# Converting the second weight chunk in two pieces, w3's rows ahead of w_out's, in a fused attention and feed-forward kernel

## The chip, the cores and the metric

The kernel runs on one core of a Trainium2 chip. The metric is the device time of one execution in microseconds (us). "Before" is the kernel without the change, "after" the kernel with it.

## The reference, cut to what matters

```python
# attention: q, k, v of 8 x 8 x 576 x 64
kv  = einsum('bhsd,bhse->bhde', k, v)
out = einsum('bhsd,bhde->bhse', q, kv)
out = out / sqrt(mean(out*out, -1) + 1e-6) * g_norm
x   = out rearranged to (4608, 512)
# feed-forward: w1, w2 (512, 1024); w3 (1024, 1024); w_out (1024, 512)
h = ((x @ w1) * (x @ w2)) @ w3
return h @ w_out
```

The weights arrive as 64-bit floats and are converted to fp32 on the chip.

## The kernel before, as far as it matters here

The kernel first folds w3 and w_out into one matrix, so that the last two products become one. It does so in two halves of w3's rows. In the first half it walks through eight chunks. One chunk is 512 columns of raw w3 data and 512 of raw w_out data per partition, loaded by two transfers of 512 KB, w3 first. Per chunk:

1. **Conversion.** ScalarE does two operations (L147, L148), VectorE four (L150, L154, L157, L160).
2. **Transpose of w3's part** on TensorE (L443) and its copy out of PSUM by ScalarE (L448).
3. **Fold** on TensorE (L456): four products of the transposed w3 with w_out, seen as eight passes in the profile. Three of the products (six passes) stand ahead of the next chunk's transpose, the fourth behind it.

TensorE, ScalarE and VectorE each work through their operations in the order in which the program was written.

```python
    def conversion(n, dst, raw, cols=slice(0, 1024)):
        # ... (views of the two 32-bit halves of each value)
        nc.scalar.activation(low, lo, AF.Copy, scale=2.0 ** -51, bias=2.0)      # L147
        nc.scalar.activation(dst, hi.bitcast(FP32), AF.Abs)                     # L148
        yield
        nc.vector.scalar_tensor_tensor(...)                                     # L150
        nc.vector.tensor_scalar(out=dst, in0=dst, scalar1=LEAST, scalar2=MOST,  # L154
                                op0=ALU.max, op1=ALU.min)
        nc.vector.tensor_scalar(...logical_shift_left)                          # L157
        nc.vector.tensor_tensor(out=dst_bits, in0=dst_bits, in1=low_bits, ...)  # L160
    # ...
    def conversions(n):
        # ...
        dst = chunks[:, i].rearrange("p w f -> p (w f)")   # w3's 512 columns, then w_out's
        cuts = [0, 1024] if i else [0, 256, 512, 1024]
        return [conversion(n, dst, raws[n], slice(a, b)) for a, b in zip(cuts, cuts[1:])]
    # begin_next(): the ScalarE part of the next chunk; end_next(): its VectorE part
    # ...
        keep_warm(14)              # matmuls on the identity, so that TensorE is not idle
        begin_next()
        end_next()                 # chunk 0
        turn_w3(0, 0)              # transposes L443, copy L448
        keep_warm(5)
        begin_next()               # chunk 1
        # ...
        for c in range(KF):
            if c == 0:
                end_next()         # chunk 1
                begin_next()       # chunk 2
            else:
                begin_next()
                end_next()
            # ...
            fold_chunk(0, c, range(NH - 1))
            turn_w3(*((0, c + 1) if c + 1 < KF else (1, 0)))
            fold_chunk(0, c, [NH - 1])
```

## Time and profile before

| | before |
|---|---|
| median of the first 3 runs | 814.15 us (813.13 to 815.48) |
| span of the profiled execution | 811.6 us |
| TensorE busy | 803.0 us (99%) |
| VectorE, ScalarE busy | 363.6 us, 266.8 us |
| TensorE's longest wait | 2.73 us, for the conversion of chunk 1 |

The prediction shows the lines for this. One view that it does not show is the chain of work that ended last, followed back from the end of the program. These are its pieces around the wait (start us, duration us, what):

```profile
3.27 6.86 DMA raw<-in_moe_w_out_dram
...
10.21 1.14 ACT ab L147
11.37 1.23 DVE ab L150
...
13.96 1.24 DVE chunks L160
...
15.24 0.66 PE at L443 x4
```

The chain runs from chunk 1's w_out transfer through its conversion into the transpose. From 15.24 on it is TensorE alone. In what follows **"the third transpose batch"** is the one of chunk 2, at 19.25 us here. It is a good marker: from it to the end of the span this profile takes 811.6 - 19.25 = 792.35 us.

### The profile page before, as it was taken

To read this page: it belongs to the slowest core of one execution; us is meant where nothing else is said; L and a number is where in the kernel's file an instruction comes from. 1 tells how busy PE (TensorE), PEld (TensorE's weight loads), DVE (VectorE), ACT (ScalarE), POOL (GpSimd) and SP (SyncE) were. 2 spreads that over 40 slices of the span, in tenths; PEclk is the share of its full clock that TensorE was granted. 3 is DMA by queue.
4 is the path that set the end of the run, shared out by engine and by line. 5 is a ranking of instruction groups with operands and counts; after the bars stand their busy time and mean duration, and the time that the engine had idled before them with its cause. 6 is when DMAs were issued, how large, how long until landed. Compare 5 with 4: busy or idle time off the path is not lost.

```text
span 811.6 us, 12588 instructions
## 1 busy us (share of the span) xinstructions
PE 803.0 (99%) x5335; PEld 676.8 (83%) x5335; DVE 363.6 (45%) x680; ACT 266.8 (33%) x501; POOL 1.8 (0%) x8
## 2 busy tenths in 40 slices
PE   7999999999999999999999999999999999999998
PEld 5455788888888888888888888888888888888887
DVE  6958998324522453155315531543154415422431
ACT  6677743124312431233124322331234212211220
POOL 0000000000000000000000000000000000000000
PEclk9999999999999999999999999999999999999999
DMA  9996433032003210312032202120210010002001
GB/s 322 332 328 182 146 91 92 1 131 82 10 1 130 75 31 1 119 47 56 1 103 67 66 1 85 56 82 0 79 52 1 1 52 1 0 1 53 1 0 53
DMA packets 60811, 59.53 MB, mean 73 GB/s; under 512 B 15316, under 2 KB 57300, under 8 KB 60756
## 3 DMA queue, kind: packets, MB, share of 16 engines
q1 hardware_dynamic: 60608, 58.60, 23.2%
q8 instruction: 42, 0.69, 0.4%
q14 instruction: 13, 0.11, 0.0%
q10 hardware_dynamic: 148, 0.13, 0.0%
HBM read 49.28 MB, written 9.44 MB: 72 GB/s over the span
## 4 chain that ended last, share of the span: by engine, by line
PE 98%; DMA 1%; DVE 0%; SPq 0%; ACT 0%; issue 0%; ACTq 0%
PE mm L471 81%; PE mm L456 7%; PE at L275 3%; PE at L345 2%; PE at L294 2%; PE at L378 2%; DMA raw<-in_moe_w_out_dram 1%; PE at L443 1%; PE at L363 0%; SPq L183 0%; PE at L387 0%; PE at L304 0%; DVE chunks L160 0%; DVE ab L150 0%; ACT ab L147 0%
## 5 line engine op out<-in xcount | busy, mean ns | idle before, releaser
L471 PE MATMUL mm<-xT,w_sb 128*128 128x256 f32 x768 | 176.2, 379 | 0.0
L471 PEld LDWEIGHTS mm<-xT,w_sb 128*128 128x128 f32 x768 | 146.0, 190 | 20.2 <-issue 0.5
L471 PE MATMUL mm<-xc,ws 128*128 128x256 f32 x576 | 130.2, 379 | 0.0
L471 PEld LDWEIGHTS mm<-xc,ws 128*128 128x128 f32 x576 | 109.5, 190 | 14.8
L484 ACT COPY u<-mm 128x512 f32<-128x512 f32 x90 | 52.7, 585 | 206.0 <-PE mm L471 185.9
L484 ACT COPY p<-mm 128x512 f32<-128x512 f32 x90 | 52.7, 586 | 134.4 <-PE mm L471 134.4
L471 PE MATMUL mm<-w3o_sb,ab 128*128 128x256 f32 x432 | 96.2, 379 | 0.0
L597 DVE TENSOR_TENSOR c<-mm,u 128x512 f32<-128x512 f32 x36 | 24.8, 689 | 157.3 <-PE mm L471 157.3
L471 PEld LDWEIGHTS mm<-w3o_sb,ab 128*128 128x128 f32 x432 | 82.1, 190 | 11.1
L471 PE MATMUL mm<-xc,w_sb 128*128 128x256 f32 x288 | 68.9, 382 | 0.0
L471 PE MATMUL mm<-raw 128*128 128x256 f32 x288 | 63.6, 379 | 0.0
L471 PE MATMUL mm<-xT,ws 128*128 128x256 f32 x256 | 61.6, 383 | 0.0
L471 PEld LDWEIGHTS mm<-raw 128*128 128x128 f32 x288 | 54.8, 190 | 7.4
L456 PE MATMUL mm<-chunks,ab 128*128 128x512 f32 x128 | 60.0, 601 | 0.2 <-DVE chunks L160 0.2
L471 PEld LDWEIGHTS mm<-xc,w_sb 128*128 128x128 f32 x288 | 52.8, 190 | 6.9 <-ACT u L484 0.3
L471 PEld LDWEIGHTS mm<-xT,ws 128*128 128x128 f32 x256 | 46.7, 190 | 6.0
L314 DVE TENSOR_REDUCE inv<-sq 128x8 f32<-128x512 f32 (+1 forms) x40 | 23.5, 626 | 58.4 <-ACT sq L313 58.4
L598 DVE TENSOR_TENSOR ab<-c 128x256 f32<-128x256 f32 x108 | 45.4, 421 | 2.9
L638 DVE TENSOR_TENSOR raw<-mm,u 128x512 f32<-128x512 f32 x8 | 5.5, 692 | 83.4 <-PE mm L471 72.7
L456 PEld LDWEIGHTS mm<-chunks,ab 128*128 128x128 f32 x128 | 21.9, 190 | 21.6 <-issue 16.1
L597 DVE TENSOR_TENSOR c<-p,u 128x512 f32<-128x512 f32 x36 | 24.9, 691 | 28.4 <-ACT u L484 28.1
L471 PE MATMUL mm<-w3o_sb,raw 128*128 128x256 f32 x144 | 32.7, 380 | 0.0
(90 smaller groups left out, 769.3 us busy)
## 6 DMA issues: line engine op xcount, KB each, us to landing
raw<-in_moe_w_dram SPq DMA_DIRECT2D x31, 512.0 KB, 7.0
k_sb<-in_k_dram SPq DMA_DIRECT2D x32, 256.0 KB, 3.9
v_sb<-in_v_dram SPq DMA_DIRECT2D x32, 256.0 KB, 4.4
q_sb<-in_q_dram SPq DMA_DIRECT2D x32, 256.0 KB, 4.5
out_dram<-raw SPq DMA_DIRECT2D x14, 512.0 KB, 2.6
raw<-in_moe_w_out_dram SPq DMA_DIRECT2D x7, 512.0 KB, 7.7
out_dram<-raw SPq DMA_DIRECT2D x9, 128.0 KB, 2.4
kl_sb<-in_k_dram SPq DMA_DIRECT2D x8, 128.0 KB, 4.8
```

What stands on the lines that cost most here:

```text
L275: nc.tensor.matmul(kv_ps[e * D:(e + 1) * D, r - rs[0], :], lhsT=k_sb[:, e, cols] if j < J else kl[:, 2 * r + e, :], rhs=v_sb[:, e, cols] i ...
L294: nc.tensor.transpose(qt_ps[:, e, i, :], q_sb[:, e, i * P:(i + 1) * P], ident)
L314: nc.vector.tensor_reduce(out=inv[:, i], in_=sq.rearrange("p (h d) -> p h d", d=D), axis=AX.X, op=ALU.add)
L345: nc.tensor.matmul(o_ps[l][tokens, n * D:(n + 1) * D], lhsT=qT[r][rows, e, i, tokens], rhs=kv_b[rows, e, r, :], start=True, stop=True,)
L378: nc.tensor.transpose(t_ps[:, j, :], st[r // 2][:, j // 2, j % 2, m:m + 2, :], ident)
L443: nc.tensor.transpose(t_ps[:, m, :], src, ident)
L456: nc.tensor.matmul(sums_ps[half][m], lhsT=w3T[half, c][:, m, :], rhs=chunks[:, c, 1, :], start=(c == 0), stop=(c == KF - 1),)
L471: nc.tensor.matmul(ps[:, u, :], lhsT=lhsT(a_name, u, c), rhs=rhs(b_name, c),  start=(u == 0 and c == 0 and to is None), stop=(c == chunks ...
L484: nc.scalar.copy(t, ps)
L597: nc.vector.tensor_add(c, one, two)
L598: nc.vector.tensor_mul(dst, c[:, 0, :], c[:, 1, :])
L638: nc.vector.tensor_add(dst, one, two)
```

## The change

The transpose needs only w3's part of the chunk, yet the conversion waits for both transfers. The change cuts chunk 1's conversion in two, w3 first, so that the w3 piece can start one transfer earlier.

```diff
-        cuts = [0, 1024] if i else [0, 256, 512, 1024]
+        cuts = [[0, 256, 512, 1024], [0, 512, 1024], [0, 1024]][min(i, 2)]
```

## The prediction

> **What bounds the kernel now.** I read the page's span and busy shares first, then everything TensorE waited for in the whole run, then the timeline of the first 25 us by engine, then when the transfers issued there landed.
>
> ```profile
> span 811.6 us, 12588 instructions
> PE 803.0 (99%) x5335; PEld 676.8 (83%) x5335; DVE 363.6 (45%) x680; ACT 266.8 (33%) x501; POOL 1.8 (0%) x8
> ...
> PE at L443 <- DVE chunks L160: 2.7, 1, 2.7
> PE mm L256 <- POOL ident masks.py:199: 1.9, 1, 1.9
> PE mm L456 <- DVE chunks L160: 0.2, 1, 0.2
> ```
>
> The first two lines say that TensorE is the bound: 803.0 of 811.6 us. The last three are all the waits of TensorE that the trace has, with total, count and longest. One wait of 2.7 us is worth attacking: a transpose (L443) of w3 chunk 1 that waits for the last conversion step (L160) of that chunk. The granted clock is 1.00 in every stretch I read, so one stretch can be compared with another by time. After this wait TensorE has no gap to the end. So what the change saves is read from when TensorE gets going again, near 15 us; later stages can only take it back.
>
> The three engines there (start us, duration us, engine, line; idle time before it and its releaser in brackets):
>
> ```profile
> 9.70 2.81 PE L456 MATMUL mm<-chunks,ab 128*128 128x512 f32 x6 [0.22 <-DVE chunks L160]
> 15.24 0.66 PE L443 MATMUL at<-ident,chunks 128*128 128x128 f32 x4 [2.73 <-DVE chunks L160]
> 15.74 3.68 PE L456 MATMUL mm<-chunks,ab 128*128 128x512 f32 x8
> ```
> ```profile
> 8.26 0.59 ACT L448 COPY ab<-at 128x512 f32<-128x512 f32 x1 [0.37 <-PE at L443]
> 10.21 1.13 ACT L147 ACTIVATE ab<-raw 128x1024 f32<-128x1024 uint32 x1 [1.37 <-DMA raw<-in_moe_w_out_dram]
> 11.25 1.14 ACT L148 ACTIVATE chunks<-raw 128x1024 f32<-128x1024 f32 x1
> ...
> 13.02 1.14 ACT L147 ACTIVATE ab<-raw 128x1024 f32<-128x1024 uint32 x1 [0.59 <-DMA raw<-in_moe_w_out_dram]
> 14.06 1.13 ACT L148 ACTIVATE chunks<-raw 128x1024 f32<-128x1024 f32 x1
> 15.94 0.58 ACT L448 COPY ab<-at 128x512 f32<-128x512 f32 x1 [0.74 <-PE at L443]
> ```
> ```profile
> 7.34 0.69 DVE L150 SCALAR_TENSOR_TENSOR ab<-raw,ab 128x512 uint32<-128x512 uint32 x1 [0.19 <-ACT ab L147]
> ...
> 8.87 0.69 DVE L160 CUSTOM_DVE_ANT_0 chunks<-chunks,ab 128x1024 uint16<-128x1024 uint16 x1
> 11.37 1.23 DVE L150 SCALAR_TENSOR_TENSOR ab<-raw,ab 128x1024 uint32<-128x1024 uint32 x1 [1.81 <-ACT ab L147]
> ...
> 13.96 1.22 DVE L160 CUSTOM_DVE_ANT_0 chunks<-chunks,ab 128x2048 uint16<-128x2048 uint16 x1
> 15.11 1.22 DVE L150 SCALAR_TENSOR_TENSOR ab<-raw,ab 128x1024 uint32<-128x1024 uint32 x1
> ```
>
> Chunk 1's conversion starts at 10.21, when the w_out half has landed, though the transpose needs only the w3 half. ScalarE takes L147 and L148, VectorE then L150, L154, L157 and L160, to 15.18; the transpose runs at 15.24. The line to keep in view is ScalarE's at 15.94: it copies the transposed w3 chunk 1 out, it stands in ScalarE's order behind chunk 2's L147 and L148, and these had waited until 13.02 for chunk 2's own w_out.
>
> Landings, each window holding one issue (last column: us from issue to landing). The issues were at 2.79 (chunk 1, w3), 3.27 (chunk 1, w_out) and 5.26 (chunk 2, w_out):
>
> ```profile
> raw<-in_moe_w_dram SPq DMA_DIRECT2D x1, 512.0 KB, 6.0
> ...
> raw<-in_moe_w_out_dram SPq DMA_DIRECT2D x1, 512.0 KB, 6.9
> ...
> raw<-in_moe_w_out_dram SPq DMA_DIRECT2D x1, 512.0 KB, 7.7
> ```
>
> So w3 of chunk 1 lands at 8.8, its w_out at 10.2, chunk 2's w_out at 13.0.
>
> **What the Trainium skill says.** "VectorE: DVE Perf Modes", section "The TRN2 errata", has a fixed cost per instruction on VectorE and ScalarE that small tiles pay each time. The trace agrees: L150 takes 1222 ns at 1024 values and 692 at 512, so 530 are for 512 values and 162 are fixed. "PSUM — Partial Sum Buffer", section "Engine vs sequencer instructions": ScalarE's and VectorE's queues are strict FIFO. ScalarE's lines agree, L448 always follows the next chunk's L148; my result hangs on this. "TensorE: Matmul & The Clock Gate", section "HAM oscillation", warns of idle gaps above about 3.4 us; the gap here is 2.73 us and the matmuls behind it take 593 ns as those ahead, so shortening it wins no clock. "DMA: Bandwidth & Descriptors", section "Where 436 GB/s comes from", puts the port ceiling at 435 GB/s; the core moved 377 to 386 GB/s from 7.5 to 15.3 us with its DMA engines always busy, so chunk 2 will not land earlier for the asking.
>
> **The change part by part.** It adds six instructions for chunk 1 (two on ScalarE, four on VectorE) and removes none of the work. By chunk 0's piece of 512, a piece costs ScalarE 6.64 to 7.89 = 1.25 us and VectorE 7.34 to 9.56 = 2.22 us. Two pieces cost ScalarE 2.50 instead of 2.18 (10.21 to 12.39) and VectorE 4.44 instead of 3.81 (11.37 to 15.18). What it moves:
>
> 1. The w3 piece on ScalarE starts when w3 has landed (8.8) and L448 of chunk 0 is done (8.85): 8.88. VectorE can begin at 8.88 + 0.69 = 9.57, just when it is done with chunk 0 (9.56). It ends at 9.57 + 2.22 = 11.8 instead of 15.18: 3.4 us earlier.
> 2. TensorE's six passes before the transpose, issued every 0.43 us from 9.70, end near 12.3. The transpose no longer waits, and runs about 2.9 us earlier. The last quarter of chunk 0's fold follows it, to about 13.6 (0.44 + 0.86).
> 3. The w_out piece on ScalarE runs 10.2 to 11.45, on VectorE 11.7 to 13.95. It is there before it can be used.
> 4. Chunk 1's fold needs the copy L448. ScalarE is in chunk 2's conversion, which still cannot start before 13.02 and ends at 15.19. So L448 runs at 15.10 (overlapping by the usual 0.1) to 15.69 instead of 15.94 to 16.52. The weight load behind it was at 16.57, and will be at about 15.74. **Gain at this point: 0.83 us**, not 2.7. TensorE's wait becomes some 1.9 to 2.1 us (13.7 to 15.75) and changes its releaser.
> 5. Does the 0.83 survive? VectorE's chunk 2 starts at 14.17 (ScalarE's L147 done, 13.02 + 1.14) instead of 15.11, ends near 18.0; its transpose comes at 19.25 - 0.83 = 18.4. Slack 0.4, as before. Chunk 3: ScalarE could start after 15.69, its data is there near 15.8 by my estimate (1 MB per 2.8 us after chunk 2's 13.0, from the two w_out landings), so VectorE gets it at about 17.0, earlier than it is free (17.9). From there VectorE takes 3.73 us a chunk (15.11 to 18.83 to 22.57) and TensorE 3.96 (15.24, 19.25, 23.21), so VectorE only pulls ahead. Loads of later chunks land in 5 to 8 us and are issued over 10 us ahead; ScalarE shows no DMA wait after 13.02. The later work of ScalarE and VectorE is released by TensorE's own results and moves with it.
>
> Sum: -0.83 us in 812, or 0.1%. From the median 814.15: 813.3.
>
> **The rivals.** (A) The whole 2.7 us goes: 811.4. For it: only one wait of that size is on record and the diff removes its releaser. Against it: L448's place behind chunk 2's L148, which the wait list cannot show, because before the change that wait is hidden under the transpose's. (B) Nothing goes, 814.1: the 0.63 us more on VectorE would count if VectorE were the pacer, as it is nearly full from 15 to 40 us. Against it: VectorE idles 1.81 us ahead of chunk 1, and the added time falls into that; it starts chunk 2 earlier than before. (C) Chunk 2 or 3 lands later, since DMA is saturated, and takes the rest back. Chunk 2's loads are issued before anything changes, so only ordinary scatter of landings remains; half a microsecond would halve the gain. (D) Slower: I see no path for it beyond scatter.
>
> **Range and chances.** The three runs of before span 813.13 to 815.48, far more than the gain, so scatter sets the range: about 1 us around the median either way, plus half a microsecond for the mechanism. 812.0 to 814.6 covers rival B and most of A. A change of 2% is 16 us; nothing here reaches it. Faster 0.005, same 0.99, slower 0.005.
>
> **What would show it right or wrong.** The wait of L443 for L160 should be gone, and a wait of about 2 us of chunk 1's first fold matmul (L456) for ACT L448 should stand in its place. L148 of 128x512 should start near 9.5; four VectorE operations of 512 values should end near 11.8; the copy L448 of chunk 1 near 15.1; TensorE's third batch of transposes (chunk 2) near 18.4; busy time of TensorE unchanged at 803. If that third batch comes at 16.5 or 19.2, step 4 or 5 is wrong. A fold start much before 15.7 would mean that ScalarE's order is not what I read. If chunk 2's first L147 starts well off 13.02, the landing moved and the size of the gain with it.

## The result

| | before | after |
|---|---|---|
| median of 6 runs | 813.75 us (813.13 to 815.48) | 812.48 us (811.69 to 814.45) |
| span of the profiled execution | 811.6 us | 809.9 us |
| third transpose batch starts | 19.25 us | 17.53 us |
| from there to the end | 792.35 us | 792.37 us |

The ratio is 0.9984 with a 95% interval of 0.9970 to 0.9999. A ratio is the mean time of one kernel's runs over that of the other's in the same rounds, so it is not quite the ratio of the medians. By the 2% rule the two are the same. The interval just excludes 1. The last row places the whole difference of the two profiles ahead of the third transpose batch.

The chain that ended last, in the profile after:

```profile
4.58 7.44 DMA raw<-in_moe_w_out_dram
...
12.12 1.17 ACT ab L147
13.29 1.03 ACT chunks L148
14.33 0.48 ACT ab L448
...
14.85 2.84 PE mm L456 x6
```

Chunk 1's w_out and all of VectorE have left the chain. It now starts at chunk 2's w_out, runs through chunk 2's two ScalarE operations to the copy of chunk 1's transpose (L448) and then to chunk 1's fold: the order that step 4 of the prediction rests on.

ScalarE's timeline after, chunk 1's w3 piece and then the copy:

```profile
8.01 0.68 ACT L147 ACTIVATE ab<-raw 128x512 f32<-128x512 uint32 x1
8.59 0.66 ACT L148 ACTIVATE chunks<-raw 128x512 f32<-128x512 f32 x1
...
14.22 0.57 ACT L448 COPY ab<-at 128x512 f32<-128x512 f32 x1
```

TensorE's timeline after, transposes and fold of chunk 1, then the third batch:

```profile
12.11 0.60 PE L443 MATMUL at<-ident,chunks 128*128 128x128 f32 x4
...
14.85 2.84 PE L456 MATMUL mm<-chunks,ab 128*128 128x512 f32 x6 [1.28 <-ACT ab L448]
17.53 0.60 PE L443 MATMUL at<-ident,chunks 128*128 128x128 f32 x4
```

VectorE's timeline after, the end of chunk 1's w_out piece and the start of chunk 2:

```profile
12.87 0.69 DVE L160 CUSTOM_DVE_ANT_0 chunks<-chunks,ab 128x1024 uint16<-128x1024 uint16 x1
13.48 1.22 DVE L150 SCALAR_TENSOR_TENSOR ab<-raw,ab 128x1024 uint32<-128x1024 uint32 x1
```

The w3 piece starts at 8.01 instead of 10.21, and the transpose at 12.11 instead of 15.24, without a wait. The 2.73 us wait has become one of 1.28 us with another releaser. The third batch moved by 1.72 us, though, which is twice the predicted 0.83. Either the landings were different or something is missing from the account. The times scatter by more than the effect, so the experiments rest on profiles first.

### The profile page after: what moved, and what is told of

Read it like the earlier page. It is cut to its first block, busy times and chain, and to the rows that moved or that the text cites. A ratio compares the mean times of both kernels' runs of the same rounds, so it can differ in the third digit from the quotient of the medians.

```text
span 809.9 us, 12595 instructions
## 1 busy us (share of the span) xinstructions
PE 802.1 (99%) x5335; PEld 675.6 (83%) x5335; DVE 363.9 (45%) x684; ACT 266.9 (33%) x503; POOL 1.8 (0%) x8
## 4 chain that ended last, share of the span: by engine, by line
PE 98%; DMA 1%; ACT 0%; issue 0%; SPq 0%; ACTq 0%
PE mm L471 81%; PE mm L456 7%; PE at L275 3%; PE at L345 2%; PE at L294 2%; PE at L378 2%; DMA raw<-in_moe_w_out_dram 1%; PE at L443 1%; DMA raw<-in_moe_w_dram 0%; PE at L363 0%; PE at L304 0%; PE at L387 0%; ACT ab L147 0%; ACT chunks L148 0%; ACT ab L448 0%
## 5 line engine op out<-in xcount | busy, mean ns | idle before, releaser
L484 ACT COPY u<-mm 128x512 f32<-128x512 f32 x90 | 52.7, 585 | 205.8 <-PE mm L471 185.9
L484 ACT COPY p<-mm 128x512 f32<-128x512 f32 x90 | 52.7, 586 | 134.4 <-PE mm L471 134.4
```

The source lines that it names most:

```text
L484: nc.scalar.copy(t, ps)
```

## The experiments

Every batch ran on one chip and shared its runs of before. The stated runs include each kernel's profiled one.

| kernel | median us (runs) | ratio to before | runs with mean granted clock of 0.998 or less |
|---|---|---|---|
| before_again | 813.67 (6) | 0.9993 | 1 of 6 |
| after_again | 812.89 (6) | 0.9984 | 2 of 6 |
| wout_first | 814.45 (6) | 0.9993 | 4 of 6 |
| copy_early | 813.16 (6) | 0.9983 | 0 of 6 |
| copy_between | 812.70 (5) | 0.9975 | 0 of 5 |
| split_c2 | 812.56 (6) | 0.9975 | 0 of 6 |
| split_all | 814.30 (6) | 0.9999 | 0 of 6 |
| after_third | 812.52 (6) | 0.9973 | 0 of 6 |
| before_third | 814.23 (6) | 1.0000 | 3 of 6 |
| fill_before | 813.76 (5) | 0.9993 | 0 of 5 |
| fill_after | 812.82 (5) | 0.9980 | 0 of 5 |
| long_gap | 818.33 (5) | 1.0050 | 5 of 5 |

All gave correct results, and by the 2% rule all are the same as before. The 95% intervals reach 0.0012 to 0.0018 to either side of a ratio, so the ratios of 0.9973 to 0.9984 can't be told apart. "Undisturbed" below means a run with a clock of 0.999 or 1.000.

### Both kernels again: where the landings fall

No edit.

> The kernel before, unchanged, for the scatter of the transfers and of the times. Ratio 1.000 to itself, interval within 0.15%. My account says that the third batch of transposes (L443, chunk 2) starts 9.1 us after chunk 1's w_out has landed (19.25 - 10.15 in the first profile), wherever that landing falls; a landing that is earlier by 0.5 us moves everything by 0.5 us. If the 1.7 us between the two first profiles is half scatter, this profile's third batch can lie anywhere between 18.3 and 19.5. The rival, that the change itself made the transfers land earlier, wants it at 19.2 to 19.3 again.

> The changed kernel, unchanged. My account: the third batch of transposes starts 5.5 us after chunk 2's w_out has landed (17.53 - 12.02), unless VectorE is the later one; ratio to before 0.9985 to 0.9995 (gain 0.4 to 1.2 us, 0.83 expected). The rival, that the change makes transfers land earlier and is worth 1.3 to 1.7 us, wants 0.9980 to 0.9984 and the landing of chunk 2's w_out near 12.0 again.

> The changed kernel a third time, for its scatter. My account: the third batch of transposes at the later of chunk 2's w_out landing + 5.5 and the end of VectorE's chunk 2; ratio to before 0.9985 to 0.9995. The rival (worth 1.3 us or more) wants 0.998.

Measured, all taken from the timelines. The start of chunk 2's first L147 stands in for the landing of its w_out; it is up to 0.1 us after it.

| profile | chunk 2's L147 | third batch | difference |
|---|---|---|---|
| before | 13.02 | 19.25 | 6.23 |
| before_again | 13.49 | 19.73 | 6.24 |
| after | 12.12 | 17.53 | 5.41 |
| after_again | 13.09 | 18.60 | 5.51 |
| after_third | 12.95 | 18.32 | 5.37 |

Before the change the third batch hangs on chunk 1's w_out: it came 9.04 and 9.05 us after chunk 1's L147 (10.21 and 10.68), as expected. That of before_again lay at 19.73, outside the 18.3 to 19.5 that I gave, because its landings were late. Chunk 2's L147 followed chunk 1's by 2.81 us in both profiles, so it can serve as the mark for both kernels.

At equal landings the change moves the third batch by 6.23 - 5.43 (mean of three) = **0.80 us**, against 0.83 predicted. The other 0.9 us between the two first profiles is the landing, 12.12 against 13.02. after_again and after_third had 13.09 and 12.95, so the change does not bring the landing forward by that much; that rival falls. A shift of a few tenths these few profiles can't exclude. In after_third, whose landing is nearest to that of before, the copy L448 runs at 15.03 (predicted 15.1), and TensorE waits 2.33 us for it (predicted some 1.9 to 2.1).

The ratios of 0.9984 and 0.9973 were lower than the 0.9985 to 0.9995 that I expected. Both intervals (0.9968 to 1.0001 and 0.9958 to 0.9988) reach into that range, but the excess came up in every batch. It is taken up below.

### w_out's piece first: early w3, or the split?

```diff
+        pieces = list(zip(cuts, cuts[1:]))
+        if i == 1:
+            pieces.reverse()
```

> Chunk 1 in the same two pieces of 512, but w_out's piece first: same instructions, no early w3. My account (it is the early w3 piece that pays, the split alone costs): the transpose of chunk 1 waits again for L160, about 0.6 us longer than before the change (two pieces of 2.2 us against 3.8 us), so the second batch of transposes at 15.9 on the first profile's landings, and the run 0.6 us slower than before, ratio 1.0007. The rival, that it is shorter instructions or the finer semaphores that help, wants 0.999 as with the change.

TensorE's timeline (the added lines move the line numbers by three):

```profile
14.96 1.12 PE L446 MATMUL at<-ident,chunks 128*128 128x128 f32 x4 [2.23 <-DVE chunks L160]
```

The transpose waits 2.23 us for the last conversion step (L160) again, and the time is that of before. So the early w3 piece is what pays. My number for the split was a miss, however: the transpose came at 14.96, 5.10 us after chunk 1's L147 (9.86), against 15.24 - 10.21 = 5.03 in before. The split costs 0.07 us, not 0.6. VectorE's two pieces take 4.34 us (10.56 to 14.90) instead of 3.81, but VectorE can begin 0.70 us after L147 starts instead of 1.16, because L147 has half the values to do. The two nearly cancel.

Another thing in this profile was unexpected. The transposes took 1.12 us instead of 0.66, the eight passes behind them 4.83 instead of 3.68, and the granted clock was 0.50 from 15.0 to 17.5 us.

### The copy ahead of chunk 2's conversion: is L448's place the only limit?

```diff
             if c == 0:
                 end_next()
+                fold_chunk(0, 0, range(NH - 1))
+                turn_w3(0, 1)
                 begin_next()
+                fold_chunk(0, 0, [NH - 1])
+                continue
```

> The changed kernel, with the copy of chunk 1's transpose (L448) ahead of chunk 2's L147 and L148 in ScalarE's order; TensorE's and VectorE's order unchanged. My account: the fold of chunk 1 starts near 13.6 to 14.0 (TensorE no longer waits about 1.3 to 2 us for that copy), but chunk 2 then starts later on ScalarE (about 13.2) and TensorE waits for VectorE's chunk 2 at the third batch of transposes, at about 18.0 to 18.3; gain against the changed kernel nil or a loss of up to 0.5 us. The rival, that the copy alone held back the rest of the 2.7 us, wants another 1 to 2 us gained: ratio to before 0.9965.

TensorE's timeline:

```profile
13.46 3.98 PE L456 MATMUL mm<-chunks,ab 128*128 128x512 f32 x8
19.28 0.63 PE L443 MATMUL at<-ident,chunks 128*128 128x128 f32 x4 [1.84 <-DVE chunks L160]
```

The wait for the copy is gone: six passes of chunk 1's fold follow chunk 0's last two within one entry. TensorE then waits 1.84 us for chunk 2, because ScalarE gave chunk 2's L147 a start of only 14.14. The third batch comes 6.7 us after the landing of chunk 2's w_out (12.6), so about 1.2 us later than with the change (5.4 to 5.5). I had expected it at 18.0 to 18.3. A part of this is the landing of chunk 0, on which the copy now hangs: its w_out was in use at 7.29 here. Against after_again, where that was even later (7.54), the third batch is still 0.68 us later (19.28 against 18.60). The undisturbed time is also worse, 813.16 against 812.51 (below). The rival, another 1 to 2 us from the copy alone, is refuted.

### The copy between chunk 2's two ScalarE operations

```diff
         nc.scalar.activation(low, lo, AF.Copy, scale=2.0 ** -51, bias=2.0)
+        if n == 2:
+            yield
         nc.scalar.activation(dst, hi.bitcast(FP32), AF.Abs)
...
                 end_next()
                 begin_next()
+                fold_chunk(0, 0, range(NH - 1))
+                turn_w3(0, 1)
+                next(begun[2][0])
+                fold_chunk(0, 0, [NH - 1])
+                continue
```

> The changed kernel, with the copy of chunk 1's transpose (L448) between chunk 2's L147 and L148 on ScalarE, so it fills ScalarE's wait without holding up chunk 2's first VectorE operation. My account (after the change ScalarE's copy and VectorE's chunk 2 bind within 0.1 to 0.3 us of each other): the fold of chunk 1 starts 1.0 us earlier than with the change, at chunk 2's w_out landing + 1.8, but TensorE then waits for VectorE's chunk 2 at the third batch of transposes, at landing + 5.4 to 5.6: nil gain, 0.0 to 0.2 us either way. The rival, that the copy is the only limit, wants the third batch at landing + 4.5 and a further 1 us.

TensorE's timeline (the added lines move the line numbers by two):

```profile
14.53 2.84 PE L458 MATMUL mm<-chunks,ab 128*128 128x512 f32 x6 [0.98 <-ACT ab L450]
18.41 0.63 PE L445 MATMUL at<-ident,chunks 128*128 128x128 f32 x4 [1.03 <-DVE chunks L162]
```

VectorE's timeline, its second operation on chunk 2:

```profile
15.58 0.69 DVE L156 TENSOR_SCALAR chunks<-chunks 128x1024 f32<-128x1024 f32 x1 [0.31 <-ACT chunks L150]
```

With the landing at 12.86 the fold starts at +1.67 instead of after's +2.7, and all of it goes back into the next wait: the third batch is at +5.55, against +5.43 with the change. The median, 812.70 against 812.52 of after_third on the same chip, says the same. A part of this the edit makes itself: chunk 2's second ScalarE operation now stands behind the copy, and VectorE waits 0.31 us for it. So this run alone does not show how near VectorE's limit lies. The profiles of after do: VectorE's chunk 2 ended 0.23, 0.14 and 0.37 us ahead of the third batch, and where TensorE waits for it the batch starts 0.14 to 0.15 us behind it (copy_early, copy_between). That leaves 0.1, 0.0 and 0.2 us. So with the change two limits lie within some 0.2 us of each other: ScalarE's copy and VectorE's chunk 2. This is why more was not to be had by moving the copy.

### Chunk 2 in two pieces as well; all chunks in two pieces

```diff
-        cuts = [[0, 256, 512, 1024], [0, 512, 1024], [0, 1024]][min(i, 2)]
+        cuts = [[0, 256, 512, 1024], [0, 512, 1024], [0, 512, 1024], [0, 1024]][min(i, 3)]   # split_c2
+        cuts = [[0, 256, 512, 1024], [0, 512, 1024]][min(i, 1)]                              # split_all
```

> The changed kernel, with chunk 2 also in two pieces of 512. My account: chunk 2's w3 piece is ready earlier, so the third batch of transposes comes about 0.9 to 1.5 us earlier than with the change; but VectorE, now without a gap, is 0.6 us later for chunk 3, so the fourth batch (which in the changed kernel has about 0.2 to 0.5 us of slack) comes 0.1 to 0.5 us later than with it: nil or a small loss. The rival, that earlier w3 halves keep paying, wants the fourth batch 0.8 us earlier and the ratio to before near 0.9975.

> Chunks 1 to 7 all in two pieces of 512. Tests the price of the fixed costs where VectorE has no slack. My account: VectorE takes 4.26 us a chunk instead of 3.73, over TensorE's 3.96 to 3.98, so TensorE waits for L160 at every chunk; chunk 7 is converted near 8.3 + 2.1 + 7 x 4.26 = 40.2 (or 39 with early landings), TensorE's last batch of the first half some 1.5 us later than with the change, and the run 1 to 2 us slower than the changed kernel, near the kernel before or 0.5 us slower than it. The rival, that small pieces are hidden, wants the same time as the changed kernel.

split_c2, TensorE's timeline, fourth batch:

```profile
22.05 0.66 PE L443 MATMUL at<-ident,chunks 128*128 128x128 f32 x4 [0.47 <-DVE chunks L160]
```

The third batch came 4.45 us after chunk 2's second L147 (13.01 to 17.46), 1.0 us earlier than with the change. The fourth waited for VectorE and came at +9.04, against +9.36, +9.49 and +9.32 in the three profiles of after. So about 0.35 us of the 1.0 survived to there, where I expected none or a loss. It did not reach the end: from the fourth batch to the end this profile takes 788.85 us, the three of after 788.42 to 788.43. Around 89 us TensorE's weight loads wait 0.47 us for a copy on ScalarE (L484). It stands behind a conversion (L148) that had waited 0.40 us for its own data: the pattern of step 4 again, in a later stage. Whether that landing was chance, one profile can't say. The time shows no gain (812.56 against 812.52 for after_third).

In split_all TensorE's transpose batches follow each other every 4.25 us (18.15, 22.40, 26.65), against 3.96 before the change: that is VectorE's 4.26 us per chunk, so VectorE is the pacer, as expected. The median is 1.8 us above that of after_third on the same chip. The fixed cost of short operations is free only where VectorE has room.

### The granted clock

The mean granted clock of a run is near 1.000 in some runs and 0.998 or less in others, and the latter are the long ones. After the first two batches the kernel before had it in 13 of 28 runs for which the clock is recorded, after in 3 of 18. The rest asks whether TensorE's wait for chunk 1 causes it.

**before_third** (no edit), **fill_before** and **fill_after** (matmuls on the identity in the gap), **long_gap** (a longer gap):

```diff
             fold_chunk(0, c, range(NH - 1))
+            if c == 0:
+                keep_warm(14, warm)           # fill_before: ahead of chunk 1's transpose
             turn_w3(*((0, c + 1) if c + 1 < KF else (1, 0)))
             fold_chunk(0, c, [NH - 1])
+            if c == 0:
+                keep_warm(8, warm)            # fill_after: ahead of chunk 1's fold
```
```diff
+        for _ in range(5 if n == 1 else 1):   # long_gap: chunk 1's clamp five times
             nc.vector.tensor_scalar(out=dst, in0=dst, scalar1=LEAST, scalar2=MOST, op0=ALU.max, op1=ALU.min)
```

> The kernel before, a third time. So far 13 of its 28 timed runs in the two batches show a granted clock of 0.998 or less and are 1 to 3 us longer than the other 15 (median 813.6), against 3 of 18 of the changed kernel (others 812.5). Theory C: TensorE's clock is taken down for a few us after the wait for chunk 1 at 12 to 15 us, in about half of the executions of the kernel before. It wants again 3 to 8 of 16 runs with the lower clock here, and, should the profiled one be among them, the clock near 0.5 just after that wait. The rival, that the lower clock strikes anywhere and by chance alike, wants no place for it and the same frequency in all kernels.

> The kernel before, with 14 matmuls on the identity (about 1.7 us, as the kernel has at its start) ahead of the transpose of chunk 1: the wait for the conversion stays, but TensorE is idle for about 1 us of it instead of 2.7. Theory C: no run or one of 6 with a granted clock of 0.998 or less; the undisturbed time unchanged at 813.5 plus or minus 0.3, so the median falls by about 0.5 to 1 us against the kernel before with its mixed runs, ratio 0.999. The rival (chance): 2 to 3 of 6 with the lower clock, ratio 1.000.

> The changed kernel, with 8 such matmuls (about 1 us) ahead of chunk 1's fold, where it waits for the copy 1.1 to 2.3 us. Theory C: no run of 6 with the lower clock, all of 812.0 to 812.9, ratio to before 0.9975 to 0.9985. The rival (chance): some runs at 814 as in the changed kernel (3 of 18).

> The kernel before, with the clamp (L154, which may be repeated without a change of the result) five times instead of once for chunk 1: chunk 1 is ready 4 x 0.69 = 2.8 us later and TensorE's wait grows from 2.7 to about 5.5 us. Theory C: the granted clock falls in all 6 runs or 5 (0.997 to 0.998), the profile shows about 0.5 for some us after the wait, and the run is 2.8 us for the wait and 1.5 to 2 us for the clock longer than an undisturbed run of before: 817.5 to 818.3. The rival (chance): 816.3, and half the runs with the lower clock, as with before.

The profiled execution of before_third was one with the lower clock (0.998). Its stretches (the columns are the stretch, its length, busy us of TensorE, its weight loads, VectorE, ScalarE and GpSimd; then the granted clock, DMA share and GB/s):

```profile
12.50:15.00 2.50, 0.83 (x2) 0.00 (x0) 2.43 (x4) 2.01 (x2) 0.00 (x0) 1.00 1.06 377
15.00:17.50 2.50, 2.27 (x7) 1.31 (x8) 2.46 (x4) 1.75 (x4) 0.00 (x0) 0.72 1.06 376
17.50:20.00 2.50, 2.50 (x4) 0.86 (x3) 2.47 (x4) 1.12 (x2) 0.00 (x0) 0.60 1.06 377
20.00:22.50 2.50, 2.50 (x10) 1.26 (x9) 2.43 (x4) 1.00 (x2) 0.00 (x0) 1.00 1.07 376
```

Its TensorE timeline, behind the wait:

```profile
15.23 0.66 PE L443 MATMUL at<-ident,chunks 128*128 128x128 f32 x4 [1.91 <-DVE chunks L160]
15.73 5.29 PE L456 MATMUL mm<-chunks,ab 128*128 128x512 f32 x8
20.86 0.60 PE L443 MATMUL at<-ident,chunks 128*128 128x128 f32 x4
```

The transpose starts at 15.23, where the first profile of before had it. The eight passes behind it then take 5.29 us instead of 3.68, while the clock falls to 0.72 and 0.60 and recovers by 20. The third batch is 1.6 us late, and from it to the end there are 813.2 - 20.86 = 792.34 us, as ever. So this execution lost its time in one place, directly behind the wait. Cut finer, the granted clock is 0.50 from 16.10 to 19.51 here, from 14.93 to 18.34 in wout_first and from 14.77 to 21.60 in long_gap: 3.41 us, 3.41 us and twice as much, 6.83 us. Half a clock for 3.41 us costs at most 1.7 us, which is 0.2% of the span, so the mean clock becomes 0.998: 19 of the 22 disturbed runs of before show this value. From the second transpose batch to the third, the three profiles take 5.63, 5.58 and 5.60 us instead of the 4.01 of the first profile of before, so 1.57 to 1.62 us were lost each time.

long_gap, TensorE's timeline and two of its stretches:

```profile
18.17 1.11 PE L444 MATMUL at<-ident,chunks 128*128 128x128 f32 x4 [5.51 <-DVE chunks L161]
19.08 4.86 PE L457 MATMUL mm<-chunks,ab 128*128 128x512 f32 x8
```
```profile
15.00:17.50 2.50, 0.00 (x0) 0.00 (x0) 2.40 (x4) 0.20 (x1) 0.00 (x0) 0.50 1.06 377
17.50:20.00 2.50, 1.83 (x6) 1.29 (x7) 2.46 (x4) 0.68 (x2) 0.00 (x0) 0.50 0.89 317
```

The wait grew to 5.51 us as intended, and all five runs have a clock of 0.996. The third batch is at 23.77: 19.25, plus 2.93 for the later transpose (2.78 of it the longer wait), plus 1.59 of slow clock. The median is 818.33, at the upper end of what theory C expected; chance alone wanted 816.3.

fill_before, TensorE's timeline, the passes on the identity:

```profile
12.57 3.29 PE L256 MATMUL mm<-ident 128*128 128x128 f32 x28
```

No run of fill_before had the lower clock (0 of 5; the runs of before in the same rounds had it in 6 of 11, before_third in 3 of 6), and its five runs lie within 813.58 to 814.42. I had mis-sized the filling: 14 matmuls are 28 passes and 3.29 us, so they fill the whole wait and push the transpose back by about 0.2 us. This fits its median, 0.3 us above an undisturbed before, and the ratio, no better than 0.9993.

fill_after has none with the lower clock either (0 of 5), but after has it seldom, and at 812.26 to 813.31 its runs are no shorter than after's undisturbed ones. It can't be told apart from after. I found no version that beats after.

**All recorded runs together.** Sorted by the mean granted clock of the run:

| | clock 0.999 or 1.000 | clock 0.998 or less |
|---|---|---|
| before (45 runs) | 23 runs, median 813.46, mean 813.48 | 22 runs, median 815.20, mean 815.41 |
| after (18 runs) | 15 runs, median 812.51, mean 812.49 | 3 runs, median 814.45, mean 814.55 |

The other five kernels with the early w3 piece have 28 runs and none with the lower clock. The split at 0.999 was drawn after seeing the data. Where the clock was lost is known for the profiled executions only.

The means differ by 814.42 - 812.83 = 1.59 us. Of this, **0.99 us** is the difference of the undisturbed runs (the profiles gave 0.80 at equal landings), and the rest, **0.60 us**, comes from how often the clock is lost: 22/45 x 1.93 - 3/18 x 2.06 = 0.94 - 0.34.

## Why the prediction was right, and where it was not

- **Steps 1 and 2** (w3 early, transpose without a wait) held. The predicted 8.88 and 12.3 us were 8.01 and 12.11 with the early landings of that execution, 8.82 and 11.83 in after_third, and 9.16 and 13.27 in after_again, where chunk 0's w_out came late.
- **Step 3** (the w_out piece is there before it can be used) held: in after it ended on VectorE at 13.56, ahead of the fold at 14.85.
- **Step 4** (the copy L448 behind chunk 2's ScalarE work sets the fold) held by the chain, by copy_early, which removed this wait, and by copy_between, which cut it to 0.98 us. Its 0.83 us was 0.80 at equal landings.
- **Step 5** (it survives to the end) held: 792.34 to 792.40 us follow the third batch in before, after, after_again, after_third and before_third; in before_again it was 792.77, with a later wait of 0.3 us that no other profile of the two kernels has. Its slack was too generous. I gave VectorE 0.4 us at the third batch, "as before", which was 0.33 (18.92 to 19.25). It had 0.23 in after, 0.37 in after_third and in effect none in after_again (L160 ends at 18.46, the batch starts at 18.60). Step 5 let chunk 2 start on VectorE as soon as ScalarE's L147 was done. In after and after_again VectorE was still at chunk 1's w_out piece then, and began 0.2 and 0.4 us later (13.48 against 13.29, 14.65 against 14.27).
- **Rival A**, the whole 2.7 us, fell: even with the copy out of the way (copy_early), VectorE's chunk 2 takes the gain back. **Rival B** is true only where VectorE has no room (split_all). **Rival C** is true as scatter: landings moved by up to 1.4 us between profiles (12.12 to 13.49). **Rival D** was not seen.
- **The step that failed** is the sentence that "shortening it wins no clock". I had taken it from one profile with a gap of 2.73 us and an untouched clock, and from the skill's 3.4 us. The kernel before runs with the lower clock in about half of its executions (22 of 45), which are 1.9 us longer in the mean; after does so in 3 of 18. The one such execution of before that was profiled lost 1.6 us directly behind this wait, and fill_before and long_gap tie the loss to it. The lower frequency is worth 0.60 us of the mean, nearly as much as the mechanism that I predicted. The median of 812.48 stayed in the range because most runs of after are undisturbed and the range was sized by scatter; to that extent it was luck. The predicted middle, 813.3, lies 0.8 us above it.

What stays open: why the same wait costs the clock in one execution and not in the next. before kept it behind a gap of 2.73 us and before_third lost it behind 1.91; after_third kept it behind 2.33 and wout_first lost it behind 2.23. The length alone does not decide between 1.9 and 2.8 us. The skill's page on the clock gate ("TensorE: Matmul & The Clock Gate", section "What's actually happening") says that activity is judged in windows of about 3.4 us that run freely and do not start with the kernel. The lengths of the losses, 3.41 and 6.83 us, agree with that. It would make it a matter of where the gap falls: in the 3.41 us ahead of the three drops TensorE was busy for 1.50, 1.23 and 1.30 us only, while a gap that two windows share might pass. But where the windows lay in the executions that kept the clock no profile shows, and no run moved the gap alone. That after loses the clock less often because its wait is split and shorter is likewise argued, not shown; shown are the frequencies, and that the loss was in none of 5 runs with the gap of before filled and in 5 of 5 with it lengthened.

## What to carry to other kernels

When a wait for data is removed, look for the instruction that stands behind another wait in some engine's fixed order: it is hidden until the first wait goes, and it sets what the change is worth. Cut a conversion where the consumer needs only one part, once, where the engine has room; each further cut pays its fixed cost and runs into the next engine. And a short idle gap of TensorE can cost clock in a part of the executions only, so look at the granted clock of every timed run, not of the one that was profiled.

## What the Trainium skill lacked or had wrong

- "TensorE: Matmul & The Clock Gate", section "HAM oscillation — how this bites in real kernels", gives idle gaps of more than about 3.4 us as what costs the clock. Here it was lost behind waits of 1.91 us (before_third) and 2.23 us (wout_first). The lower clock came in 22 of 45 runs of before, whose profiled waits there were 1.85 to 2.73 us, and in 5 of 5 runs with a wait of 5.51 us. One loss cost 1.57 to 1.62 us in the three profiles that have it.
- No page that I drew on says how far the landing of the first transfers can scatter between executions of the same program: chunk 2's w_out was in use at 12.12, 12.95 and 13.09 us in three profiles of after, which moves the end by as much as the change does.
